# Attention, routed experts and an MLP on one core: paired bias operations, shorter GpSimd sums, and a planner that knows how TensorE's array is split

## The chip, the cores and the metric

One core of a Trainium2 chip runs the whole program in one launch. The metric is device time in microseconds (us), lower is better. Engines: PE is TensorE's matmul, PEld its weight load, DVE VectorE, ACT ScalarE, POOL GpSimd, SP SyncE (here it only issues DMAs).

## The reference

Three parts follow one another:

```python
proj = einsum('bhsd,md->bhsm', x, omega)            # x is q or k, scaled; b=4 h=8 s=576 d=64, m=128
h = proj - sum(x * x, -1, keepdims) / 2
phi = exp(h - max(h, -1, keepdims)) / sqrt(m)
kv, z = einsum('bhsm,bhsd->bhmd', phi_k, v), sum(phi_k, axis=2)
attn = einsum('bhsm,bhmd->bhsd', phi_q, kv) / (einsum('bhsm,bhm->bhs', phi_q, z)[..., None] + 1e-6)
# 2304 tokens of 512: each goes to the expert of its largest logit (8 experts, 512 -> 1024 -> 512, relu), times its gate
# then a dense layer 512 -> 2048, a piecewise quadratic, 2048 -> 512
```

## The kernel before

The program has an attention stage (to about 178 us), a sort of the tokens by expert, the experts, and the dense layers. The change lies in the first, in the step to the sort, and in one register load of the experts.

The attention stage is a list of tasks that class `Plan` puts in order when the program is built. Each task has an engine, a cost in ns, a rank, the tasks it comes after and the ring buffers it takes and uses. `run` keeps a clock for each engine and picks, again and again, the task that can start first (within `SLACK`, the lowest rank). What comes out is a fixed order for each engine; on the chip every engine works through its own in order and waits where an input is not there.

A block is 256 rows of q or k of one batch (8 heads, 2 rows a partition: 128x1024), or the last 64 rows of two batches (128x512, "small"): 20 blocks. `block_tasks` loads it, squares it (ACT for k, POOL for q), and adds up the 64 squares of each row on POOL in six halving additions (L424, L426) into `nsq`. A unit is four heads of a block: 36 units. `unit_tasks` transposes the unit (L449), copies it out of PSUM on ACT (L454), and multiplies with omega in four groups `project(c)` that use quarters of the array (64x64, L461) into two PSUM banks, one for each half `i` of the unit. For each half DVE takes the row maximum over 128 features (L468), then two small operations on 128x4 make the bias (L471, L475), and ACT runs four exponentials (L480). `kv_tasks` makes kv and z of four heads on halves of the array (64 columns, L506), `c_tasks` transposes the q features (L564), copies them and makes numerator, denominator and logits (L581, halves of the array) for a tile of 128 tokens, and `r_tasks` ranks the tokens of one or two tiles by expert, scales the rows and stores them to `xd` in HBM (L679 for the tile of the small blocks, L682 for the others). Transposes and the small ranking matmuls (L686 to L715) use the whole array. PSUM is one ring of 8 banks ("ps") for all of this.

After the plan, DVE sorts the experts by size (L856 to L896). `gather(0)` reads the rows of the first expert by index (three DMAs of POOL, L937); in the program it waits for every store to `xd` and for the index `gidx` (L724). `m_x0` transposes them, `m_split` makes two float parts on ACT and DVE, and `m_h`, `m_y` are the expert's two layers. ACT reads eight offsets from `ints` into registers (L926) ahead of the first split; each `yT` write uses one (L1002).

Of the kernel before, what the change touches and what calls it, by code (L numbers as in the profile page):

```python
# [18 lines left out]
P = 128  # L19
# [19 lines left out]
class Plan:  # L39

    SLACK = 10.0
    HOPS = {"PE": {"PE": 30.0, "ACT": 200.0, "DVE": 200.0, "POOL": 200.0, "SP": 200.0},
# [12 lines left out]

    def add(self, engine, cost, fn, rank, after=(), take=(), use=()):
        for b in use:  # L60
            b["uses"] += 1
        self.tasks.append((engine, cost, fn, rank, [a for a in after if a is not None], take, use))
        return len(self.tasks) - 1
# [4 lines left out]
    def run(self):  # L68
# [8 lines left out]
        at = {t[0]: 0.0 for t in self.tasks}  # L77
        order = []
        while open_:
            best = {}  # L80
            for i in open_:
                engine, _, _, rank, _, take, _ = self.tasks[i]
# [14 lines left out]
            start, _, i = pick  # L97
            engine, cost, fn, _, _, take, use = self.tasks[i]
            open_.remove(i)
# [56 lines left out]
def kernel(  # L156
# [144 lines left out]
    with ExitStack() as actx:  # L301
# [57 lines left out]
        def omega_tasks():  # L359
            pb = buf("ps")  # L360

            def load():
                for i in range(2):
                    nc.sync.dma_start(out=om2[:, i * HD:(i + 1) * HD], in_=omega)
                nc.sync.dma_start(out=cs[:, P:C_END], in_=consts[:, P:C_END])

            def turn():
                nc.tensor.transpose(at(pb)[:, 0, :], om2, ident)

            def scaled():  # L370
# [7 lines left out]
            x = add("PE", 110, turn, -5, after=[x], take=[pb])  # L378
            return add("ACT", 240, scaled, -5, after=[x], use=[pb])
# [15 lines left out]
        def block_tasks(which, blk, rank):  # L395
# [23 lines left out]
            def tree():  # L419
                nsq = ap.tile([P, 2 * H, 1], F32, name="nsq", tag="nsq", bufs=12)  # L420
# [6 lines left out]
                o["nsq"] = nsq[:, :, 0]  # L427

            f = 0.5 if small else 1.0
            sb = buf("sqt")  # L430
            o["load"] = add("SP", 1460 * f, load, rank - 8, take=[o["buf"]])
            if which == "k":
                t = add("ACT", 950 * f, lambda: square("ACT"), rank - 0.5, after=[o["load"]], take=[sb], use=[o["buf"]])
            else:
                t = add("POOL", 2300 * f, lambda: square("POOL"), rank - 0.5, after=[o["load"]], take=[sb],
                        use=[o["buf"]])
            o["sq"] = add("POOL", 3540 * f, tree, rank - 0.4, after=[t], use=[sb])
            return o

        def unit_tasks(u, o, rank, prev):
# [31 lines left out]
            def bias2(i):  # L474
                dve.scalar_tensor_tensor(out=r["bi", i], in0=r["sq", i], scalar=SQ, in1=r["mx", i],  # L475
                                         op0=ALU.mult, op1=ALU.subtract)

            def exps(i):
                for j in range(4):
                    act.activation(at(ppb)[:, 2 * j + i, :], at(pjb[i])[:, j, :], AF.Exp, bias=r["bi", i][:, j:j + 1])  # L480

            pjb = [buf("ps"), buf("ps")]
            ta = add("PE", 435, turn, rank - 1.5, after=[o["load"]] + prev, take=[ptb], use=[o["buf"], ptb])
# [4 lines left out]
            ends, tb = [], x  # L488
            for i in range(2):
                t = add("DVE", 600, lambda i=i: top(i), rank + 4.5, after=[tb, o["sq"]], use=[pjb[i]])  # L490
                t = add("DVE", 75, lambda i=i: bias1(i), rank + 1, after=[t])
                t = add("DVE", 75, lambda i=i: bias2(i), rank + 1, after=[t])
                ends.append(add("ACT", 1005, lambda i=i: exps(i), rank + 2, after=[t] + ends[0:1],
# [4 lines left out]
        def kv_tasks(b, hf, a, st, rank, vload):  # L498
# [38 lines left out]
            for h in range(4):  # L537
                t = add("PE", 640, lambda h=h: head(h), rank + 3 + 0.2 * h,
                        after=a[0]["done"] + a[1]["done"] + st["done"] + [vload, t], take=[kvb] if h == 0 else [],
                        use=bufs)  # L540
# [3 lines left out]
            t = add("PE", 216, turn, rank + 1.2, after=[c1], take=[p1], use=[kcb])  # L544
            t = add("ACT", 265, copy3, rank + 1.2, after=[t], take=[ktb], use=[p1])
            t = add("PE", 400, gates, rank + 1.3, after=[t, gload], take=[p2], use=[ktb])
            t = add("DVE", 100, copy4, rank + 1.3, after=[t], use=[p2])
# [3 lines left out]
        def c_tasks(t, us, kvs, rank):  # L551
# [55 lines left out]
            for hf in range(2):  # L607
                x = add("PE", 435, lambda hf=hf: turn(hf), rank + 3.5, after=done, take=[ptb[hf]], use=bufs)
                cp_.append(add("DVE" if hf else "ACT", 600 if hf else 480, lambda hf=hf: copy(hf), rank,
                               after=[x], take=[qtb[hf]], use=[ptb[hf]]))  # L610
            x = None
            for hf in range(2):
                y = add("PE", 560, lambda hf=hf: num(hf), rank + 0.5, after=[cp_[hf], x] + kvs,
                        take=[nmb[hf]], use=[qtb[hf]])
                x = add("ACT", 295, lambda hf=hf: copy_out(hf), rank + 1.5, after=[y, x], take=[] if hf else [nxb],
                        use=[nmb[hf]])
# [7 lines left out]
        def r_tasks(t0, cs_, rank, prev):  # L624
# [117 lines left out]
            for j in range(n):  # L742
# [6 lines left out]
                add("SP", 730, lambda j=j: store(j), rank - 4, after=[g], use=[xb[j]])  # L749
            x = add("PE", 35, count, rank + 0.3, after=[rs], take=[pb])  # L750
# [6 lines left out]
            x = add("PE", 142 * n, place, rank + 0.5, after=ws, take=[p2])  # L757
            places.append(x)
# [160 lines left out]
    with ExitStack() as mctx:  # L919
# [71 lines left out]
        def m_y(e, d, h):  # L991
# [3 lines left out]
            for f in range(8):  # L995
# [246 lines left out]
```

## Time and profile before

| | |
|---|---|
| time, median of 3 runs (lowest, highest) | 857.43 us (854.82, 857.69) |
| the profiled execution: its own time, span | 862.34 us, 860.5 us |
| busy: PE, PEld, DVE, ACT, POOL | 800.6, 719.0, 578.9, 360.7, 406.6 us |
| first matmul of the experts (L981) | at 191.85 us |

Busy time is what an engine's instructions cover; a busy PE is not a PE at its peak, since matmuls overlap and their ends are modelled. In the 40 slices of the profile's page PE has 8 or 9 tenths nearly everywhere but in slice 9 (172 to 194 us), which is the step from attention to the experts, and the granted clock is at five tenths there.

### The profile page before, as it was taken

What the parts mean: (1) busy time and instruction counts of PE and PEld (TensorE: products, weight loads), DVE (VectorE), ACT (ScalarE), POOL (GpSimd) and SP (SyncE); (2) the same over time, 40 slices, a digit from 0 to 9 for tenths busy, and PEclk for the clock granted to TensorE, in tenths of its full rate; (3) what the DMA queues carried; (4) which work ended last, traced back from release to release, by engine and by line L of the source; (5) the groups of instructions that cost most, each with busy time, mean ns of one, the idle gap of its engine ahead of it and who ended that gap; (6) DMA issues with size and microseconds to landing.
All of it is one profiled execution on the core that took longest, in us unless ns stands there. A gap on an engine that the chain in (4) does not pass through costs nothing.

```text
span 860.5 us, 17028 instructions
## 1 busy us (share of the span) xinstructions
PE 800.6 (93%) x6530; PEld 719.0 (84%) x6530; DVE 578.9 (67%) x1174; ACT 360.7 (42%) x890; POOL 406.6 (47%) x467
## 2 busy tenths in 40 slices
PE   6898999759999999979979999999999999999994
PEld 4676777629999999969869898999989999899993
DVE  3789996965557654634598776589667977746541
ACT  5887978602222222211244645444343344434321
POOL 6868782443444444152265543355344544333443
PEclk9999999959999999999999999999999999999998
DMA  9966201135555555474442111012001200001111
GB/s 221 219 156 169 88 36 28 51 108 170 156 172 170 177 161 171 84 173 147 150 156 90 50 37 38 26 50 74 26 25 50 74 26 1 1 13 50 50 49 62
DMA packets 79025, 80.72 MB, mean 94 GB/s; under 512 B 28896, under 2 KB 61792, under 8 KB 78932
## 3 DMA queue, kind: packets, MB, share of 16 engines
q1 hardware_dynamic: 74996, 68.10, 28.2%
q0 software_dynamic: 3120, 9.85, 3.4%
q10 hardware_dynamic: 816, 1.57, 0.5%
q8 instruction: 54, 0.88, 0.4%
q14 instruction: 39, 0.32, 0.1%
HBM read 70.06 MB, written 9.45 MB: 92 GB/s over the span
## 4 chain that ended last, share of the span: by engine, by line
PE 45%; DVE 3%; DMA 1%; issue 1%; POOL 1%; ACT 0%; POOLq 0%; DVEq 0%; SPq 0%; ACTq 0%
PE po L1181 8%; PE ph L1137 7%; PE ph L1135 7%; PE ph L1136 7%; PE po L1180 7%; PE po L1179 7%; DVE wy L260 1%; DVE yl L916 1%; DMA out_dram<-acc,oidx 1%; DMA wraw<-in_moe_w_dram 0%; POOL gl L1164 0%; DMA wraw<-in_moe_w_in_dram 0%; DVE wy L259 0%; DVE wl L274 0%; DVE wz L263 0%
## 5 line engine op out<-in xcount | busy, mean ns | idle before, releaser
L1164 POOL TENSOR_TENSOR gl<-cl,gh 128x384 fp32r<-128x384 f32 x96 | 102.6, 1091 | 161.9 <-ACT gh L1163 151.9
L1156 ACT ACTIVATE cl<-cl,half 128x384 f32<-128x384 f32 x96 | 56.9, 614 | 211.2 <-DVE cl L1155 211.2
L265 POOL TENSOR_SCALAR wh<-wraw 128x1024 fp32r<-128x1024 f32 x60 | 70.2, 1173 | 138.3 <-DMA wraw<-in_moe_w_dram 86.6
L1136 PE MATMUL ph<-yl,wh 128*128 128x384 f32 x384 | 128.9, 336 | 1.8 <-DVE yl L916 1.8
L1137 PE MATMUL ph<-yh,wl 128*128 128x384 f32 x384 | 129.0, 336 | 0.0
L1135 PE MATMUL ph<-yh,wh 128*128 128x384 f32 x384 | 128.9, 336 | 0.0
L1181 PE MATMUL po<-wh,gl 128*128 128x512 f32 x288 | 113.6, 394 | 0.5 <-POOL gl L1164 0.5
L1180 PE MATMUL po<-wl,gh 128*128 128x512 f32 x288 | 113.0, 392 | 0.0
L1179 PE MATMUL po<-wh,gh 128*128 128x512 f32 x288 | 112.2, 389 | 0.0
L1155 DVE TENSOR_SCALAR cl<-ph 128x384 f32<-128x384 f32 x96 | 51.4, 551 | 77.1 <-PE ph L1137 76.3
L274 DVE TENSOR_TENSOR wl<-wraw,wh 128x1024 fp32r<-128x1024 f32 x60 | 75.3, 1255 | 17.3 <-POOL wh L265 17.3
L981 PE MATMUL ph<-xh,wh 128*128 128x328 f32 (+7 forms) x256 | 81.4, 318 | 5.6 <-DVE hl L987 3.6
L480 ACT ACTIVATE pp<-ps,bi 128x128 f32<-128x128 f32 x288 | 82.1, 407 | 6.0 <-DVE bi L475 6.0
L916 DVE TENSOR_TENSOR yl<-yT,yh 128x384 fp32r<-128x384 f32 x96 | 80.9, 900 | 4.3 <-ACT yh L915 4.3
L999 PE MATMUL py<-hh,wh 128*128 128x328 f32 (+7 forms) x256 | 81.2, 317 | 1.7 <-ACT yT L1002 1.7
L982 PE MATMUL ph<-xl,wh 128*128 128x328 f32 (+7 forms) x256 | 80.0, 313 | 2.8 <-DVE xl L950 2.8
L1000 PE MATMUL py<-hl,wh 128*128 128x328 f32 (+7 forms) x256 | 78.4, 306 | 2.5 <-DVE hl L987 2.5
L983 PE MATMUL ph<-xh,wl 128*128 128x328 f32 (+7 forms) x256 | 79.6, 311 | 0.0
L1001 PE MATMUL py<-hh,wl 128*128 128x328 f32 (+7 forms) x256 | 78.6, 307 | 0.2 <-DVE wl L274 0.2
L1136 PEld LDWEIGHTS ph<-yl,wh 128*128 128x128 f32 x384 | 72.1, 188 | 3.9 <-DVE yl L916 2.1
L1135 PEld LDWEIGHTS ph<-yh,wh 128*128 128x128 f32 x384 | 72.2, 188 | 1.8
L1137 PEld LDWEIGHTS ph<-yh,wl 128*128 128x128 f32 x384 | 72.1, 188 | 0.0
(158 smaller groups left out, 1700.5 us busy)
## 6 DMA issues: line engine op xcount, KB each, us to landing
wraw<-in_moe_w_dram SPq DMA_DIRECT2D x57, 512.0 KB, 3.8
wraw<-in_moe_w_in_dram SPq DMA_DIRECT2D x16, 512.0 KB, 4.1
wraw<-in_moe_w_out_dram SPq DMA_DIRECT2D x16, 512.0 KB, 3.4
xd<-xr SPq DMA_DIRECT2D x17, 256.0 KB, 2.3
blk<-in_k_dram SPq DMA_DIRECT2D x8, 512.0 KB, 6.8
blk<-in_q_dram SPq DMA_DIRECT2D x8, 512.0 KB, 5.0
vm<-in_v_dram SPq DMA_DIRECT2D x16, 256.0 KB, 5.8
wra<-in_moe_w_dram SPq DMA_DIRECT2D x4, 512.0 KB, 4.8
```

What stands on the lines that cost most here:

```text
L480: act.activation(at(ppb)[:, 2 * j + i, :], at(pjb[i])[:, j, :], AF.Exp, bias=r["bi", i][:, j:j + 1])
L916: nc.vector.tensor_sub(yl, yT[d][:, c], yh.bitcast(F32))
L981: nc.tensor.matmul(ph, lhsT=wh[:, d, c], rhs=xh, start=(d == 0), stop=False)
L982: nc.tensor.matmul(ph, lhsT=wh[:, d, c], rhs=xl, start=False, stop=False)
L999: nc.tensor.matmul(py, lhsT=wh[:, a, c], rhs=hh, start=(f == 0), stop=False)
L1135: nc.tensor.matmul(ph[f], lhsT=wh[:, a, c], rhs=yh, start=(d == 0), stop=False)
L1136: nc.tensor.matmul(ph[f], lhsT=wh[:, a, c], rhs=yl, start=False, stop=False)
L1137: nc.tensor.matmul(ph[f], lhsT=wl[:, a, c], rhs=yh, start=False, stop=(d == 3))
L1164: nc.gpsimd.tensor_sub(gl, cl, gh.bitcast(F32))
L1179: nc.tensor.matmul(po, lhsT=gh[:, c], rhs=wh[:, a, :], start=(f == 0), stop=False)
L1180: nc.tensor.matmul(po, lhsT=gh[:, c], rhs=wl[:, a, :], start=False, stop=False)
L1181: nc.tensor.matmul(po, lhsT=gl[:, c], rhs=wh[:, a, :], start=False, stop=(f == 3))
```

## The change

Five edits. (1) The two maxima of a unit go into one 128x2x4 tile, and one pair of bias operations on 128x8 serves both halves; the exponentials of the first half now come after the maximum of the second. The sum of squares is awaited by the bias, and no longer by the maxima. (2) POOL makes only the first two halvings of the squares (64 to 16); a DVE sum over 16 (`total`) makes the rest. (3) Each PE task names its mode, "whole", "halves" or "quarters" of the array; the planner adds 95 ns where the mode changes. Some costs are new. (4) The tile of the small blocks is stored with two DMAs of 64 rows in place of one with two pieces of 64 rows. (5) The offsets are loaded one by one, just ahead of the first `yT` write of each expert but the first, whose offset is 0.

```diff
+    CHANGE = 95.0
-                start = max(at[engine], ready[i])
+                start = max(at[engine] + (self.CHANGE if mode and mode != now else 0.0), ready[i])
...
             def tree():
-                w = 32
-                while w > 1:
+                for w in (32, 16):
                     pool.tensor_add(t[:, :, 0:w], t[:, :, 0:w], t[:, :, w:2 * w])
-                    w //= 2
-                pool.tensor_add(nsq[:, 0:n, :], t[:, :, 0:1], t[:, :, 1:2])
+            def total():
+                o["nsq"] = ap.tile([P, 2 * H], F32, name="nsq", tag="nsq", bufs=12)
+                dve.reduce_sum(o["nsq"][:, 0:n], at(sb)[:, 0:n, 0:16], axis=AX)
...
-            o["sq"] = add("POOL", 3540 * f, tree, rank - 0.4, after=[t], use=[sb])
+            t = add("POOL", 2000 * f, tree, rank - 0.4, after=[t], use=[sb])
+            o["sq"] = add("DVE", 60 + 270 * f, total, rank - 0.3, after=[t], use=[sb])
...
-            def bias1(i):
-                dve.scalar_tensor_tensor(out=r["mx", i], in0=r["sq", i], scalar=SQ, in1=r["mx", i],
-                                         op0=ALU.mult, op1=ALU.add)
...
+            def bias():
+                sq = o["nsq"][:, 8 * hf:8 * hf + 8].rearrange("p (j i) -> p i j", i=2)
+                dve.scalar_tensor_tensor(out=r["mx"], in0=sq, scalar=SQ, in1=r["mx"], op0=ALU.mult, op1=ALU.add)
+                dve.scalar_tensor_tensor(out=r["bi"], in0=sq, scalar=SQ, in1=r["mx"], op0=ALU.mult, op1=ALU.subtract)
...
-                x = add("PE", 240, lambda c=c: project(c), rank + 1 + 0.1 * c, after=[x, setup],
-                        take=[] if c else pjb, use=[thb] + pjb)
+                x = add("PE", 220, lambda c=c: project(c), rank + 1 + 0.1 * c, after=[x, setup],
+                        take=[] if c else pjb, use=[thb] + pjb, mode="quarters")
...
-                    rows = xd[2 * it[1] * S:(2 * it[1] + 2) * S, :].rearrange("(i s) d -> i s d", i=2)
-                    nc.sync.dma_start(out=rows[:, 512:576, :], in_=x)
+                    for i in range(2):
+                        o = (2 * it[1] + i) * S + 512
+                        nc.sync.dma_start(out=xd[o:o + 64, :], in_=x[64 * i:64 * i + 64])
...
-        offs = [nc.scalar.value_load(ints[0:1, 0, e:e + 1], min_val=0, max_val=NT) for e in range(E)]
+        offs = {}
...
-            nc.scalar.activation(yT[d][:, bass.ds(offs[e], w)], py, AF.Copy)
+            if e and d == 0:
+                offs[e] = nc.scalar.value_load(ints[0:1, 0, e:e + 1], min_val=0, max_val=NT)
+            nc.scalar.activation(yT[d][:, bass.ds(offs[e], w)] if e else yT[d][:, 0:w], py, AF.Copy)
```

On PE, where the first batch's kv is made (ps are PSUM banks, vm and vs hold v, pp the k features, th a transposed unit; L506 is kv, L461 is projection), the order before is:

```order
L449 MATMUL ps_102<-cs,blk_114 128x128 x4
L506 MATMUL ps_101<-vm_148,pp_122 64x65 x4
L506 MATMUL ps_101<-vm_148,pp_124 64x65 x4
L506 MATMUL ps_101<-vs_150,pp_123 64x65 x2
L461 MATMUL ps_103<-oms,th_120 64x128
L461 MATMUL ps_102<-oms,th_120 64x128
L461 MATMUL ps_103<-oms,th_120 64x128
L461 MATMUL ps_102<-oms,th_120 64x128
L506 MATMUL ps_101<-vm_148,pp_122 64x65 x4
```

At the same place the order now is (kv is L508, the transpose of a unit L454):

```order
L454 MATMUL ps_104<-cs,blk_113 128x128 x4
L508 MATMUL ps_108<-vm_148,pp_122 64x65 x4
L508 MATMUL ps_108<-vm_148,pp_124 64x65 x4
L508 MATMUL ps_108<-vs_150,pp_123 64x65 x2
L508 MATMUL ps_108<-vm_148,pp_122 64x65 x4
L508 MATMUL ps_108<-vm_148,pp_124 64x65 x4
L508 MATMUL ps_108<-vs_150,pp_123 64x65 x2
```

The kv of a head alternated with a quarter of a projection; now the eight heads of both halves stand in one run. Over the attention stage PE's order has 202 changes of mode before and 76 now.

On DVE, the first two units of the program before (mx and bi are the maxima and the biases):

```order
L468 TENSOR_REDUCE mx<-ps_104 128x4
L468 TENSOR_REDUCE mx<-ps_105 128x4
L471 SCALAR_TENSOR_TENSOR mx<-nsq,mx 128x4 x2
L475 SCALAR_TENSOR_TENSOR bi<-nsq,mx 128x4 x2
L468 TENSOR_REDUCE mx<-ps_106 128x4
L468 TENSOR_REDUCE mx<-ps_107 128x4
L471 SCALAR_TENSOR_TENSOR mx<-nsq,mx 128x4 x2
L475 SCALAR_TENSOR_TENSOR bi<-nsq,mx 128x4 x2
```

and now:

```order
L431 TENSOR_REDUCE nsq<-sqt_116 128x16
L473 TENSOR_REDUCE mx<-ps_103 128x4
L431 TENSOR_REDUCE nsq<-sqt_117 128x8
L473 TENSOR_REDUCE mx<-ps_104 128x4
L477 SCALAR_TENSOR_TENSOR mx<-nsq,mx 128x8
L478 SCALAR_TENSOR_TENSOR bi<-nsq,mx 128x8
L473 TENSOR_REDUCE mx<-ps_106 128x4
L473 TENSOR_REDUCE mx<-ps_107 128x4
L477 SCALAR_TENSOR_TENSOR mx<-nsq,mx 128x8
L478 SCALAR_TENSOR_TENSOR bi<-nsq,mx 128x8
```

Four small operations of a unit became two, and the sums of squares of a block (L431) entered DVE's queue.

On SP, the last stores to xd before:

```order
L682 DMA xd<-xr_143 128x512
L682 DMA xd<-xr_141 128x512
L682 DMA xd<-xr_142 128x512
L679 DMA xd<-blk_111 2x64x512
```

and now:

```order
L685 DMA xd<-xr_143 128x512
L685 DMA xd<-xr_141 128x512
L685 DMA xd<-xr_142 128x512
L682 DMA xd<-blk_109 64x512 x2
```

Only the last store changed its shape.

## Rows read from the trace of the kernel before

**Rows 1.** Busy time by stage: start and end us, then each engine, PEclk, DMA share, GB/s.

```profile
20.00:158.00 138.00, 126.93 (x2471) 99.80 (x2471) 116.78 (x373) 117.67 (x379) 91.97 (x149) 0.99 0.45 111
158.00:178.00 20.00, 11.51 (x211) 9.38 (x210) 18.83 (x97) 7.84 (x24) 11.72 (x21) 0.85 0.25 95
178.00:192.00 14.00, 7.57 (x27) 3.65 (x25) 6.38 (x40) 0.64 (x2) 5.81 (x6) 0.62 0.30 86
192.00:860.50 668.50, 642.92 (x3672) 597.26 (x3672) 431.16 (x650) 224.39 (x465) 285.02 (x257) 0.99 0.28 87
```

**Rows 2.** Waits of PE from 20 to 158 us: total us, times, longest.

```profile
PE ps L581 <- DVE qt L570: 1.8, 1, 1.8
...
PE ps L461 <- DVE kvz L530: 0.4, 1, 0.4
```

**Rows 3.** Timeline of PE at two places: start us, us, instruction, count.

```profile
65.56 1.10 PE L461 MATMUL ps<-oms,th 64*64 64x128 f32 x32
66.59 0.18 PE L686 MATMUL ps<-rsb,oneb 128*128 128x16 bf16 x1
...
106.12 0.45 PE L461 MATMUL ps<-oms,th 64*64 64x128 f32 x8
106.50 0.73 PE L581 MATMUL ps<-kvz,qt 128*64 128x73 f32 x16
107.16 0.45 PE L461 MATMUL ps<-oms,th 64*64 64x128 f32 x8
```

**Rows 4.** Groups by line to 215 us: busy us, mean ns, idle before and releaser.

```profile
L468 DVE TENSOR_REDUCE mx<-ps 128x4 f32<-128x512 f32 x72 | 47.7, 681 | 16.7 <-PE ps L461 15.1 <-ACT kvt L522 1.2 <-issue 0.3
...
L475 DVE SCALAR_TENSOR_TENSOR bi<-nsq,mx 128x4 f32<-128x4 f32 x72 | 23.0, 338 | 0.2
L471 DVE SCALAR_TENSOR_TENSOR mx<-nsq,mx 128x4 f32<-128x4 f32 x72 | 22.5, 330 | 1.0 <-POOL nsq L426 1.0
...
L424 POOL TENSOR_TENSOR sqt<-sqt 128x128 f32<-128x128 f32 x20 | 10.0, 500 | 1.6
...
L602 DVE TENSOR_REDUCE lall<-lg 128x8 f32<-128x64 f32 x18 | 4.7, 263 | 0.3
```

**Rows 5.** Timeline of POOL and DVE around 105 us.

```profile
104.47 2.06 POOL L671 TENSOR_TENSOR xr<-nx,den 128x512 f32<-128x512 f32 x2 [0.56 <-DVE mx L471]
...
105.47 0.15 DVE L471 SCALAR_TENSOR_TENSOR mx<-nsq,mx 128x4 f32<-128x4 f32 x1
...
105.65 0.90 DVE L475 SCALAR_TENSOR_TENSOR bi<-nsq,mx 128x4 f32<-128x4 f32 x1
```

**Rows 6.** DMA from 170 to 190 us: GB/s in 0.5 us slices; stores, us to landing.

```profile
GB/s 0 0 0 0 0 287 238 287 238 0 209 315 0 0 25 25 45 12 33 49 41 49 57 49 66 49 41 0 0 0 0 0 0 123 336 115 213 221 123 180
...
xd<-xr SPq DMA_DIRECT2D x3, 256.0 KB, 2.0
```

**Rows 7.** Timeline from the last store to the first split of the experts.

```profile
176.00 0.52 SPq L679 DMA_DIRECT2D xd<-blk  x1
...
178.05 0.16 DVE L724 TENSOR_TENSOR gidx<-slots,ps 128x3 uint32<-128x3 f32 x1 [0.42 <-PE ps L854]
...
184.66 1.18 POOL L937 DMA_INDIRECT xg<-xd,gidx  x1 [7.90 <-DVE tsi L892]
...
184.83 0.18 DVE L896 CAST spos<-tsi 128x36 f32<-128x36 int32 x1
...
191.36 0.44 ACT L949 ACTIVATE xh<-px 128x328 fp32r<-128x328 f32 x1 [17.65 <-PE px L943]
```

**Rows 8.** ACT's offset loads: ns least, median, most; first and last start.

```profile
L926 ACTq TENSOR_LOAD <-ints x8: 277/280/477, 181.1 to 185.3; - x8
```

**Rows 9.** Timeline of ACT in the second expert: a write of yT.

```profile
242.01 0.40 ACT L1002 ACTIVATE yT<-py 128x272 f32 x1 [3.36 <-PE py L1001]
```

**Rows 10.** Busy time from 70 to 80 us, columns as in Rows 1.

```profile
70.00:80.00 10.00, 7.23 (x114) 5.78 (x116) 8.74 (x19) 6.57 (x19) 9.22 (x15) 0.83 0.72 182
```

**Rows 11.** Timeline of PE at 76 us.

```profile
76.00 0.79 PE L581 MATMUL ps<-kvz,qt 128*64 128x73 f32 x16 [1.76 <-DVE qt L570]
```

More of the change, by code (lines that the diff above doesn't have):

```diff
@@ L57, in buf, with add @@
         return {"ring": ring, "uses": 0, "end": 0.0}
-    def add(self, engine, cost, fn, rank, after=(), take=(), use=()):
+    def add(self, engine, cost, fn, rank, after=(), take=(), use=(), mode=None):
         for b in use:
             b["uses"] += 1
-        self.tasks.append((engine, cost, fn, rank, [a for a in after if a is not None], take, use))
+        self.tasks.append((engine, cost, fn, rank, [a for a in after if a is not None], take, use, mode))
         return len(self.tasks) - 1
@@ L78, in run @@
         order = []
+        now = None
         while open_:
@@ L81, in run @@
             for i in open_:
-                engine, _, _, rank, _, take, _ = self.tasks[i]
-                start = max(at[engine], ready[i])
+                engine, _, _, rank, _, take, _, mode = self.tasks[i]
+                start = max(at[engine] + (self.CHANGE if mode and mode != now else 0.0), ready[i])
                 for ring in {b["ring"] for b in take}:
@@ L97, in run @@
             start, _, i = pick
-            engine, cost, fn, _, _, take, use = self.tasks[i]
+            engine, cost, fn, _, _, take, use, mode = self.tasks[i]
+            now = mode or now
             open_.remove(i)
@@ L377, in omega_tasks @@
             add("DVE", 130, tri, 1, after=[x])
-            x = add("PE", 110, turn, -5, after=[x], take=[pb])
+            x = add("PE", 110, turn, -5, after=[x], take=[pb], mode="whole")
             return add("ACT", 240, scaled, -5, after=[x], use=[pb])
@@ L434, in block_tasks @@
             else:
-                t = add("POOL", 2300 * f, lambda: square("POOL"), rank - 0.5, after=[o["load"]], take=[sb],
+                t = add("POOL", 1900 * f, lambda: square("POOL"), rank - 0.5, after=[o["load"]], take=[sb],
                         use=[o["buf"]])
-            o["sq"] = add("POOL", 3540 * f, tree, rank - 0.4, after=[t], use=[sb])
+            t = add("POOL", 2000 * f, tree, rank - 0.4, after=[t], use=[sb])
+            o["sq"] = add("DVE", 60 + 270 * f, total, rank - 0.3, after=[t], use=[sb])
             return o
@@ L478, in exps @@
             def exps(i):
                 for j in range(4):
-                    act.activation(at(ppb)[:, 2 * j + i, :], at(pjb[i])[:, j, :], AF.Exp, bias=r["bi", i][:, j:j + 1])
+                    act.activation(at(ppb)[:, 2 * j + i, :], at(pjb[i])[:, j, :], AF.Exp, bias=r["bi"][:, i, j:j + 1])
             pjb = [buf("ps"), buf("ps")]
-            ta = add("PE", 435, turn, rank - 1.5, after=[o["load"]] + prev, take=[ptb], use=[o["buf"], ptb])
+            ta = add("PE", 435, turn, rank - 1.5, after=[o["load"]] + prev, take=[ptb], use=[o["buf"], ptb], mode="whole")
@@ L489, in unit_tasks @@
             for i in range(2):
-                t = add("DVE", 600, lambda i=i: top(i), rank + 4.5, after=[tb, o["sq"]], use=[pjb[i]])
-                t = add("DVE", 75, lambda i=i: bias1(i), rank + 1, after=[t])
-                t = add("DVE", 75, lambda i=i: bias2(i), rank + 1, after=[t])
+                t = add("DVE", 600, lambda i=i: top(i), rank + 4.5, after=[t], use=[pjb[i]])
+            t = add("DVE", 150, bias, rank + 1, after=[t, o["sq"]])
+            for i in range(2):
                 ends.append(add("ACT", 1005, lambda i=i: exps(i), rank + 2, after=[t] + ends[0:1],
@@ L537, in kv_tasks @@
             for h in range(4):
-                t = add("PE", 640, lambda h=h: head(h), rank + 3 + 0.2 * h,
+                t = add("PE", 570, lambda h=h: head(h), rank + 3 + 0.2 * h,
                         after=a[0]["done"] + a[1]["done"] + st["done"] + [vload, t], take=[kvb] if h == 0 else [],
-                        use=bufs)
+                        use=bufs, mode="halves")
                 heads.append(t)
@@ L543, in kv_tasks @@
             c2 = add("ACT", 270, copy2, rank + 1, after=[t], use=[kvb])
-            t = add("PE", 216, turn, rank + 1.2, after=[c1], take=[p1], use=[kcb])
+            t = add("PE", 216, turn, rank + 1.2, after=[c1], take=[p1], use=[kcb], mode="whole")
             t = add("ACT", 265, copy3, rank + 1.2, after=[t], take=[ktb], use=[p1])
-            t = add("PE", 400, gates, rank + 1.3, after=[t, gload], take=[p2], use=[ktb])
+            t = add("PE", 400, gates, rank + 1.3, after=[t, gload], take=[p2], use=[ktb], mode="whole")
             t = add("DVE", 100, copy4, rank + 1.3, after=[t], use=[p2])
@@ L607, in c_tasks @@
             for hf in range(2):
-                x = add("PE", 435, lambda hf=hf: turn(hf), rank + 3.5, after=done, take=[ptb[hf]], use=bufs)
+                x = add("PE", 435, lambda hf=hf: turn(hf), rank + 3.5, after=done, take=[ptb[hf]], use=bufs, mode="whole")
                 cp_.append(add("DVE" if hf else "ACT", 600 if hf else 480, lambda hf=hf: copy(hf), rank,
@@ L612, in c_tasks @@
             for hf in range(2):
-                y = add("PE", 560, lambda hf=hf: num(hf), rank + 0.5, after=[cp_[hf], x] + kvs,
-                        take=[nmb[hf]], use=[qtb[hf]])
+                y = add("PE", 510, lambda hf=hf: num(hf), rank + 0.5, after=[cp_[hf], x] + kvs,
+                        take=[nmb[hf]], use=[qtb[hf]], mode="halves")
                 x = add("ACT", 295, lambda hf=hf: copy_out(hf), rank + 1.5, after=[y, x], take=[] if hf else [nxb],
@@ L677, in store @@
                 if it[0] == "s":
-                    rows = xd[2 * it[1] * S:(2 * it[1] + 2) * S, :].rearrange("(i s) d -> i s d", i=2)
-                    nc.sync.dma_start(out=rows[:, 512:576, :], in_=x)
+                    for i in range(2):
+                        o = (2 * it[1] + i) * S + 512
+                        nc.sync.dma_start(out=xd[o:o + 64, :], in_=x[64 * i:64 * i + 64])
                 else:
@@ L749, in r_tasks @@
                 add("SP", 730, lambda j=j: store(j), rank - 4, after=[g], use=[xb[j]])
-            x = add("PE", 35, count, rank + 0.3, after=[rs], take=[pb])
+            x = add("PE", 60, count, rank + 0.3, after=[rs], take=[pb], mode="whole")
             x = add("DVE", 95, mine, rank + 2.3, after=[x], use=[pb])
@@ L756, in r_tasks @@
                 ws.append(add("DVE", 330, lambda j=j: one_b(j), rank + 0.4, after=[x, places[-1]]))
-            x = add("PE", 142 * n, place, rank + 0.5, after=ws, take=[p2])
+            x = add("PE", 160 * n, place, rank + 0.5, after=ws, take=[p2], mode="whole")
             places.append(x)
```

17 lines of the change are left out of this document (6 added, 11 removed).

## The prediction

> **What bounds the kernel now.** I read the busy time by stage first, then the waits of each engine in the attention stage, then single stretches of the timeline, and last the step from attention to the experts, wait by wait.
>
> From 192 us on PE is busy 642.92 of 668.50 us [rows 1], and no edit touches its work there. What the change can move is how early that part starts. From 20 to 158 us three engines are near each other: PE 126.93 of 138 us (92%), ACT 117.67 (85%), DVE 116.78 (85%), with POOL at 91.97 (67%) [rows 1]. PE waits little: twelve groups of waits, from 1.8 us down to 0.4, sum to 11.5 us [rows 2]. So PE is the queue that sets the pace, and ACT and DVE are 20 us behind it. From 158 to 178 us DVE is the bound, 18.83 of 20 us, on the ranking of the last tiles [rows 1]. From 178 to 192 us nearly nothing works: the last store is issued at 176.00, the index is written at 178.05, and the first gather starts at 184.66 [rows 7]. The row names DVE L892 as what it waited for, but the program lets it wait for the stores and for L724, which is long done. The store is still moving: in half-microsecond slices the three stores before it go at 209 to 315 GB/s, and then a trickle of 12 to 57 GB/s lasts for thirteen slices, from 177.0 to 183.5 [rows 6]. That trickle is the 256 KB of L679.
>
> **The change, part by part.**
>
> *Mode changes on PE.* A run of 32 projection loads takes 66.59 - 65.56 = 1.03 us to the next kind; a run of 8 takes 106.50 - 106.12 = 0.38 [rows 3]. Both hold one change c at their end, so with a for 8 loads 4a + c = 1.03 and a + c = 0.38: a = 0.22, c = 0.16. The order goes from 202 changes to 76, so PE is relieved of 126 x 0.15 = 18.9 us (0.15 to round down, since a change into the small ranking matmuls is cheaper). Bounds: 0.10 gives 12.6, 0.16 gives 20.2.
>
> *Bias and sums on DVE.* 144 operations of 338 and 330 ns go, 45.5 us [rows 4]. 72 on 128x8 come. The same operation takes 0.15 us where GpSimd leaves it alone and 0.90 beside a GpSimd multiplication [rows 5], and a mean of 0.33 is mostly that wait, so I price the new ones at 0.33: 23.8 us (bounds 0.15 and 0.34: 11 and 24.5). 20 sums over 16 come; no row has 128x256 into 16, and the neighbours are 263 ns for 64 elements and 681 for 512 [rows 4]. In proportion to elements that is 0.44 for 16 of them and 0.32 for the 4 small ones, 8.4 us (bounds 5.3 and 13.6). Net DVE -13 us. It buys no time by itself while PE sets the pace; it keeps DVE (to about 104) from taking PE's place.
>
> *GpSimd's levels.* The four short levels go, the largest of them 10.0 us [rows 4], some 25 us in all by the same group of lines. POOL has a third of the stage free, so this is priced at nothing; the cover is that free time. The new wait is the bias on the sum, and what stands behind a late sum is DVE's whole queue, the maxima of the next unit first. Before, that wait cost 1.0 us in all, once [rows 4]; with POOL less loaded I take 0.
>
> *Later exponentials.* The first half's exponentials now wait for the second maximum, 0.68 us, and the bank is held that much longer. With 36 units and two banks each that is some 0.4 us a bank more on about 4, against eight banks. Price 0 in the forecast; it is the seed of the slow rival.
>
> *What the attention stage gains.* If PE kept its 11.5 us of waits, the stage would shrink by the whole 18.9. But ACT's 117.67 us stay. The highest share that any engine holds in this stage is PE's 92%; at that share ACT needs 117.67 / 0.92 = 128 us. I take that: 138 to 128, -10 us. The ends are -18.9 and -2.
>
> *The tail of the stage.* Counted in PE's order, after the last projection there stood 6 groups of q transposes and 9 of numerators; now 10 and 14. That is work put off to where DVE and not PE is the bound: 9 groups at about 0.5 us (a group of 16 takes 107.16 - 106.50 = 0.66 with its change [rows 3]), 4.5 us if none hides, 0 if all does. I take +2.
>
> *The store.* The nearest row for a store that is one piece per row is xd<-xr, 2.0 us to landing [rows 6]. The second half is issued after the first, 0.52 us later at most [rows 7]: 176.0 + 0.5 + 2.0 = 178.5, against the end of the trickle at 183.5. The gather came 1.16 us after that end, so now at 179.7, 5.0 us earlier; no earlier than the index allows, so 5.4 at best, and 0 at worst if 64 rows move like two times 64. I take 4.5, with half a microsecond off because the gather's descriptors are now written while DVE sorts (to 184.83 + 0.18 [rows 7]).
> The trace has no store of 64 rows, so it can't say on how many DMA engines one spreads. The Trainium skill, "DMA: Bandwidth & Descriptors", "Why a DMA increments its semaphore by 16 and not by 1", says that the number of engines is the largest up to 16 that divides the slowest dimension of both sides: 2 for a target of 2x64 rows, 16 for 64. The trickle at a sixth of the other stores' rate agrees with the 2; by the rule the halves go like xr's stores, and the sum takes the 5.0, without it 0.
> What is late next is the split of the first expert: ACT's first xh at 191.36 waited 17.65 us for PE [rows 7], and moves with the gather.
>
> *The offset loads.* Eight of them, one every (185.3 - 181.1) / 7 = 0.6 us, held ACT from 181.1 to 185.6 or later [rows 8], inside that wait. With the gather 4.5 us earlier the first xh is due at 186.9, so leaving them there would still have just fit: 0 gained. Seven come back in the experts, ahead of a yT write that waits 3.36 us for PE [rows 9], which hides one of 0.6 us: 0. If the cover were gone, 7 x 0.6 = 4.2.
>
> *Sum.* -10 + 2 - 4.5 = -12.5 us on the profiled execution's 862.34 (1.8 more than its span): 849.8. That execution lies 0.6% above the median of the runs shown, 857.43, so the forecast in their terms is 857.43 x 849.8 / 862.34 = 845.
>
> **Rivals.**
>
> *PE alone was the limit (15%).* ACT and DVE waited for PE, not on their own account, and close up fully: -18.9 + 2 - 4.5 = -21.4, 836. For it: DVE's maxima wait 15.1 us on PE's projections, much of it at the start [rows 4]. Against it: ACT would have to be busy 117.67 of 119 us.
>
> *The gather doesn't come earlier (12%).* Either the halves are as slow as the whole, or descriptors starve while DVE sorts. -10 + 2 = -8: 849.5. For it: every gather of the trace but its first 0.2 us lay outside the sort, so none shows the overlap. The Trainium skill's "SBUF — State Buffer", "Who interferes with whom", speaks for this one: a DVE instruction in its two-port modes locks GpSimd out for its whole length, and descriptors of GpSimd's DMAs can't be written meanwhile. In this trace the sort's instructions take 0.15 to 0.3 us each, so by the rule the gather is delayed in short steps, at most to the sort's end at 185.0, where the 5.0 us would be gone.
>
> *The order brings nothing (8%).* Fixed queues of ACT and DVE, filled from costs, stay as loosely coupled as now: stage -2, tail +2, store -4.5: 853.
>
> *Long runs starve the other engines: slower (5%).* PE now makes kv of eight heads or two whole units in one run, and holds its banks longer. Where PE waited 1.76 us for DVE at 76.00 [rows 11], the granted clock fell to half soon after: 0.83 on average from 70 to 80 us [rows 10], so 0.17 x 10 x 2 = 3.4 us ran at 1.2 GHz and cost 1.7 us more. One such event costs 1.8 + 1.7 = 3.5 us. The gains are 18.9 + 4.5, less 2; from the seventh event on it is slower, and there are some 18 pairs of units in which it can happen. Eight give 862. Against it: so far it happens once in 138 us, with DVE fuller than it will be.
>
> **How the numbers follow.** The forecast has 60%. Its own range is 841 to 850: the stage between -6 and -14. At the start of the experts some 4 us run at half clock now; shifted, that is 2 us either way. To hold 8 in 10 the range reaches from 834, just past the first rival, to 855, past the third. Half a per cent, 4.3 us, is about what a measurement of this kernel tells from none, so faster means under 853.1: all of the forecast, the first two rivals and half of the third, less something for what I have not thought of: 0.86. Within half a per cent: 0.09. Slower: 0.05.
>
> **What would show it.** Mode changes: PE's busy time up to the end of the projections falls by 15 to 19 us. Stage: the last projection starts about 10 us earlier, and ACT's share rises past 90%; if PE's waits grow by much more than 9 us, ACT or the banks have taken over. Bias: L477 and L478 together near 24 us, the sums near 8. Store: no trickle after it, the first gather 1 to 2 us behind the index. Offsets: the loads inside waits of ACT for PE. Experts: from the first L984 to the end 668 to 670 us as now. The prediction is wrong if that last part changes by more than 3 us, or if the clock falls more than twice before the last projection.

## The result, and the profile after

The changed kernel takes 844.81 us (median of 4 runs, 841.62 to 849.25) against 857.56 us (4 runs, 854.82 to 859.41) for the kernel before: a ratio of 0.9853, 95% interval 0.9807 to 0.9899. The profiled execution took 845.65 us, its span 843.9; 845 was predicted.

The stages, with the stretches of [rows 1] (start and end us, then each engine, PEclk, DMA share, GB/s):

```profile
20.00:158.00 138.00, 120.10 (x2582) 105.20 (x2574) 116.00 (x359) 120.29 (x393) 74.62 (x88) 0.98 0.45 115
158.00:178.00 20.00, 10.46 (x95) 6.03 (x95) 16.39 (x95) 2.17 (x7) 11.41 (x17) 0.66 0.35 114
178.00:192.00 14.00, 12.94 (x75) 12.56 (x76) 6.88 (x11) 3.68 (x9) 5.03 (x6) 0.88 0.58 189
```

The stretch from 178 to 192 us, in which PE had 7.57 us of work, is now filled: the experts have begun. From the end of the last store on, the timeline answers to [rows 7]:

```profile
168.19 1.09 SPq L682 DMA_DIRECT2D xd<-blk  x2
169.39 0.16 DVE L727 TENSOR_TENSOR gidx<-slots,ps 128x3 uint32<-128x3 f32 x1 [0.42 <-PE ps L857]
...
172.10 1.17 POOL L940 DMA_INDIRECT xg<-xd,gidx  x1 [3.64 <-DVE u L871]
...
176.17 0.18 DVE L899 CAST spos<-tsi 128x36 f32<-128x36 int32 x1
...
178.92 0.44 ACT L952 ACTIVATE xh<-px 128x328 fp32r<-128x328 f32 x1 [12.98 <-PE py L946]
179.41 0.42 PE L984 MATMUL ph<-xh,wh 128*128 128x328 f32 x1 [0.47 <-ACT xh L952]
```

The index comes 8.7 us earlier (178.05 to 169.39), the first gather 12.6 us (184.66 to 172.10), the first matmul of the experts 12.44 us (191.85 to 179.41). The gather follows the index by 2.71 us, where it was 6.61, and runs while DVE still sorts.

All engines before and after, cut just behind the start of the last projection (156.36 us before, 142.15 now) and at the index, columns as in [rows 1]; first before, then after:

```profile
0.00:156.50 156.50, 137.68 (x2607) 107.95 (x2607) 121.00 (x382) 126.75 (x398) 103.35 (x182) 0.99 0.52 126
156.50:178.00 21.50, 12.48 (x239) 10.12 (x227) 20.33 (x104) 8.87 (x28) 12.42 (x23) 0.86 0.23 88
```

```profile
0.00:142.40 142.40, 119.52 (x2511) 104.08 (x2511) 112.55 (x317) 119.83 (x377) 80.17 (x102) 0.98 0.58 138
142.40:169.40 27.00, 18.09 (x330) 15.25 (x323) 23.87 (x119) 14.62 (x49) 11.90 (x23) 0.82 0.19 71
```

The projections end 14.2 us earlier, but the rest of the stage grew from 21.5 to 27 us: 5.6 us of PE's work and 5.75 of ACT's now lie behind the last projection.

The groups that the change touches on DVE, to 180 us, answer to [rows 4] (busy us, mean ns, idle before and releaser):

```profile
L473 DVE TENSOR_REDUCE mx<-ps 128x4 f32<-128x512 f32 x72 | 46.8, 681 | 7.3 <-PE ps L466 7.2
L477 DVE SCALAR_TENSOR_TENSOR mx<-nsq,mx 128x8 f32<-128x8 f32 x36 | 12.7, 353 | 0.3
...
L478 DVE SCALAR_TENSOR_TENSOR bi<-nsq,mx 128x8 f32<-128x8 f32 x36 | 11.8, 328 | 1.2
...
L431 DVE TENSOR_REDUCE nsq<-sqt 128x16 f32<-128x256 f32 (+1 forms) x20 | 7.6, 384 | 8.4 <-POOL sqt L427 8.4
```

The biases take 24.5 us and the sums 7.6. New is what stands behind the last bar: DVE waits 8.4 us for GpSimd ahead of the sums, where it waited 1.0 us before.

### The profile page after: what moved, and what is told of

It is laid out like the page before. It is cut to its first block, busy times and chain, and to the rows that moved or that the text cites. A ratio compares the mean times of both kernels' runs of the same rounds, so it can differ in the third digit from the quotient of the medians.

```text
span 843.9 us, 16906 instructions
## 1 busy us (share of the span) xinstructions
PE 786.3 (93%) x6530; PEld 719.0 (85%) x6530; DVE 577.7 (68%) x1122; ACT 359.9 (43%) x890; POOL 379.0 (45%) x387
## 4 chain that ended last, share of the span: by engine, by line
PE 47%; DVE 3%; DMA 1%; POOL 1%; issue 1%; ACT 0%; POOLq 0%; DVEq 0%; ACTq 0%
PE po L1186 8%; PE ph L1142 8%; PE ph L1140 8%; PE ph L1141 8%; PE po L1185 7%; PE po L1184 7%; DVE wy L265 1%; DVE yl L919 1%; DMA out_dram<-acc,oidx 1%; DMA wraw<-in_moe_w_in_dram 1%; PE ph L984 0%; PE ph L985 0%; PE ph L986 0%; POOL gl L1169 0%; DVE wy L264 0%
## 5 line engine op out<-in xcount | busy, mean ns | idle before, releaser
L270 POOL TENSOR_SCALAR wh<-wraw 128x1024 fp32r<-128x1024 f32 x60 | 67.5, 1126 | 137.8 <-DMA wraw<-in_moe_w_dram 85.9
L482 ACT ACTIVATE pp<-ps,bi 128x128 f32<-128x128 f32 x288 | 84.3, 472 | 6.6 <-DVE bi L478 6.6
```

## The experiments

Each kernel was timed over five rounds beside the kernel before. "Ratio" is to that kernel; "index" is the start of `gidx`, "clock" PE's mean granted clock from 20 to 140 us, both from the one profiled execution.

| kernel | ratio (95%) | index, us | clock |
|---|---|---|---|
| before | 1 | 178.05 | 0.99 |
| after | 0.9853 (0.9807 to 0.9899) | 169.39 | 0.97 |
| s1: after, one store | 0.9906 (0.9872 to 0.9940) | 169.31 | 0.96 |
| s2: before, two stores | 0.9927 (0.9905 to 0.9948) | 178.98 | 0.97 |
| m2: after, edit 3 undone | 0.9924 (0.9901 to 0.9947) | 176.01 | 0.97 |
| m3: before, edit 3 alone | 0.9978 (0.9954 to 1.0002) | 176.14 | 0.93 |
| b1: after, edit 2 undone | 0.9941 (0.9920 to 0.9963) | 179.42 | 0.93 |
| b2: after, edit 1 undone | 0.9914 (0.9888 to 0.9939) | 173.15 | 0.97 |
| o1: after, edit 5 undone | 0.9848 (0.9825 to 0.9872) | 173.07 | 0.94 |
| m4: after, 150 ns a change | 0.9914 (0.9880 to 0.9947) | 174.56 | 0.93 |
| m5: after, 110 ns a change | 0.9942 (0.9917 to 0.9967) | 174.87 | 0.97 |
| f1: after's order, two biases | 0.9892 (0.9853 to 0.9931) | 172.13 | 0.96 |
| f2: after's order, GpSimd sums | 0.9963 (0.9944 to 0.9982) | 176.91 | 0.91 |
| f3: after's order, one level | 0.9880 (0.9849 to 0.9911) | 168.91 | 0.94 |

A tenth of a per cent is 0.86 us.

### The store: s1 and s2

```diff
-                    for i in range(2):
-                        o = (2 * it[1] + i) * S + 512
-                        nc.sync.dma_start(out=xd[o:o + 64, :], in_=x[64 * i:64 * i + 64])
+                    rows = xd[2 * it[1] * S:(2 * it[1] + 2) * S, :].rearrange("(i s) d -> i s d", i=2)
+                    nc.sync.dma_start(out=rows[:, 512:576, :], in_=x)
```

s1 is this on the kernel after; s2 is the reverse on the kernel before.

> The kernel after, with the tile of the small blocks stored by one DMA with two pieces of 64 rows again (edit 4 undone), all else kept; the order of PE is the same. Theory: the slow trickle comes back, some 7 us from its issue at about 168.2 us to 175.5, and the first gather starts 1.2 us behind it, at 176.7 in place of 172.1: 844.8 + 4.6 = 849.4 us. Rival (the gather was early because the stage before it was shorter, and the store is hidden beside the sort): the gather stays near 172 to 173, 845 us.

> The kernel before, with edit 4 alone. Theory: no trickle, both halves land within 3 us of 176.0, the first gather at 179.2 to 179.7 in place of 184.66: 857.6 - 5 = 852.6 us. Rival (GpSimd's descriptors cannot be written while DVE sorts the experts, so the gather still starts near 185): 857.6 us.

Measured: s1 0.9906, 4.6 us above after; the two intervals overlap, so that here the traces decide. The DMA of s1 and then of after, in half-microsecond slices from 165 us:

```profile
GB/s 0 0 0 0 0 274 250 0 25 16 41 16 33 45 41 49 49 57 49 49 49 4 0 0 0 0 0 106 246 189 156 254 139 164 90 131 287 156 164 262
```

```profile
GB/s 0 0 0 0 0 217 307 0 106 184 213 21 0 0 0 0 0 25 156 320 98 123 303 82 172 123 156 270 148 246 189 127 188 369 377 365 348 385 397 381
```

In s1 the trickle is back, 16 to 57 GB/s from 169.0 to 175.5 us, and the gather starts at 176.81; after, the same bytes are through in four slices. In s1's trickle (169.0 to 175.5 us) the DMA share is 0.12, worth about two engines of 16; in after's four slices it is 0.59. The index is the same (169.31, 169.39), so the 4.5 us between the first matmuls of the experts (183.94, 179.41) are the store's alone. s2 gains 0.7%, 6.3 us, with 4.5 to 8.2 in the interval; in its profile the gather follows the index by 1.86 us (178.98, 180.84) while the sort goes on. Both rivals, hidden store and starved descriptors, fall.

### The order of PE: m2 and m3

m2 sets `CHANGE` to 0 and PE's costs to those of before; m3 is the kernel before with edit 3 alone:

```diff
-    CHANGE = 95.0
+    CHANGE = 0.0
...
-                x = add("PE", 220, lambda c=c: project(c), rank + 1 + 0.1 * c, after=[x, setup],
+                x = add("PE", 240, lambda c=c: project(c), rank + 1 + 0.1 * c, after=[x, setup],
```

> The kernel after, with edit 3 undone (no price for a change of mode, PE's costs of before): 195 changes of mode in PE's order in place of 76; edits 1, 2, 4, 5 stay. Theory (the stage got shorter because PE changes mode less often): PE's busy time to the last projection rises by 119 x 0.15 = 18 us, the index comes 8 to 9 us later, near 178, time 844.8 + 8.7 = 853.5 us. Rival (the relief of DVE and GpSimd by edits 1 and 2 made the stage shorter): the index stays near 170, 845 to 847 us.

> The kernel before, with edit 3 alone (71 changes of mode in place of 202); bias, sums, store and offset loads as before. Theory: PE is relieved by 131 x 0.15 = 19.6 us and the index comes 8 to 9 us earlier, near 169.5; the store's trickle stays: 857.6 - 8.7 = 848.9 us. Rival (without the relief of DVE and GpSimd these two hold the stage where it is): 855 to 858 us.

Measured: m2 0.9924, m3 0.9978. Without edit 3 the time is 6.1 us above after, where the theory had 8.7. But m2 equals s2 (0.9924, 0.9927): edits 1, 2 and 5, in the order that the planner makes without edit 3, bring nothing beyond the store. And edit 3 alone brings 1.9 us, not 8.7, in an interval that includes 1: the rival. That PE has less to do in the new order is shown; that it is through sooner is not. From 20 to 140 us, m2, after and m3:

```profile
20.00:140.00 120.00, 110.81 (x2164) 87.29 (x2158) 96.81 (x273) 103.47 (x331) 63.29 (x69) 0.97 0.50 123
20.00:140.00 120.00, 104.66 (x2269) 91.89 (x2262) 100.78 (x295) 105.44 (x344) 69.45 (x76) 0.97 0.51 127
20.00:140.00 120.00, 103.44 (x2150) 90.57 (x2150) 96.44 (x303) 101.94 (x333) 85.87 (x139) 0.93 0.49 123
```

At the same clock of 0.97, after does 105 matmuls more than m2 in 6.15 us less of PE's time. In these 120 us the kernel before has 109.46 us of PE at a clock of 0.99. m3 needs 6 us less for as many instructions (2152 and 2150), but 0.07 of 120 us, 8.4 us of full-speed work, is missing in its clock, against 1.2 before and 3.6 after. PE's waits, the longest of m3:

```profile
PE ps L720 <- DVE ob L712: 3.7, 2, 3.1
PE ps L691 <- ACT pp L485: 1.9, 1, 1.9
PE ps L466 <- DVE kvz L535: 1.8, 1, 1.8
```

So the order relieves PE, and in m3 PE stands idle more than before (16.6 us of the 120, against 10.5) and runs at half clock more often. But after has 15.3 us of idle PE too, and f3 below ends level with after at a clock of 0.94, so neither alone shows why m3 gains so little; that stays open. Store (0.73%), order (0.22%) and relief (0) alone make 0.95%; together they make 1.5%.

### Which relief: b1 and b2, and the planner's part: m4 and m5

b1 puts all six levels of the sum back on GpSimd, b2 puts two bias operations back for each half, both with the planner's costs of these steps as before, so that the order is planned anew. m4 and m5 change one number:

```diff
-    CHANGE = 95.0
+    CHANGE = 150.0
```

> The kernel after, with all six levels of the sums on GpSimd again (edit 2 undone, the paired bias stays); 72 changes of mode. DVE has 8 us less to do, GpSimd 25 us more. Theory P (what lets the new order of PE pay is DVE's relief by the pairing): nothing is lost, ratio to before 0.984 to 0.988. Theory S (GpSimd's short levels slow DVE's small operations and hold the bias): the mean of the bias operations rises above the 0.34 us of after, and half of the 6 us that edit 3 lacked without help is lost: ratio 0.989 to 0.994.

> The kernel after, with two bias operations for each half again (edit 1 undone, the sums split between GpSimd and DVE as after); 75 changes of mode. DVE has 72 operations of 0.33 us more, 22 to 24 us. Theory P: DVE becomes the queue that PE waits for, the granted clock falls more often, and the gain of the order is gone: ratio 0.991 to 0.995. Theory S: the pairing is worth nothing: ratio 0.984 to 0.988.

> The kernel after, with 150 ns for a change of mode in the planner in place of 95 (the 0.15 us that the prediction took as its real cost); 71 changes in place of 76. Theory (the planner gains by true costs): 5 x 0.15 = 0.75 us less for PE and a plan that drifts less, ratio 0.982 to 0.985. Rival (the order is sensitive: any other order of the same quality moves the index by some microseconds): a ratio between 0.983 and 0.993, with the granted clock at half in other places.

> The kernel after, with 110 ns for a change of mode in the planner in place of 95: 77 changes in place of 76, the order differs from about the fortieth part of the stage on. Theory L (two orders of equal quality by the planner's own measure lie up to 6 us apart on the chip, so that the 0.985 of after is in part luck): a ratio of 0.987 to 0.993. Rival (orders of equal count are equal, and 150 ns was worse because of its longer runs): 0.984 to 0.987.

Measured: b1 0.9941, b2 0.9914, m4 0.9914, m5 0.9942. b1 and b2 alone would say that each relief is needed (theory P is out for b1, theory S for b2). But m4 and m5 have every edit and as few changes of mode (71 and 77, where after has 76), and lose 5.2 and 7.7 us all the same. The planner's order is one draw among many, and draws of equal count differ by as much as the parts that were to be told apart. So the losses of b1 and b2 can't be put down to their edits. Nor can the 6.1 us between m2 and after, or the little that m3 gains, be put down to edit 3, since m2 and m3 were planned anew too: what the new order of PE is worth in time, no run here shows. Parts can be told apart only by kernels that keep the order.

### The same order: f1, f2 and f3

Here every task keeps its place; only what stands inside the bias or the sum differs. f1 makes the biases of the halves apart:

```diff
-                dve.scalar_tensor_tensor(out=r["mx"], in0=sq, scalar=SQ, in1=r["mx"], op0=ALU.mult, op1=ALU.add)
+                for i in range(2):
+                    dve.scalar_tensor_tensor(out=r["mx"][:, i, :], in0=sq[:, i, :], scalar=SQ, in1=r["mx"][:, i, :],
+                                             op0=ALU.mult, op1=ALU.add)
```

f2 makes `tree` six levels again and `total` empty; f3 goes the other way:

```diff
-                for w in (32, 16):
-                    pool.tensor_add(t[:, :, 0:w], t[:, :, 0:w], t[:, :, w:2 * w])
+                pool.tensor_add(t[:, :, 0:32], t[:, :, 0:32], t[:, :, 32:64])
...
-                dve.reduce_sum(o["nsq"][:, 0:n], at(sb)[:, 0:n, 0:16], axis=AX)
+                dve.reduce_sum(o["nsq"][:, 0:n], at(sb)[:, 0:n, 0:32], axis=AX)
```

> The kernel after, with exactly its order of tasks on every engine; only inside the bias step of a unit the pair of operations on 128x8 is again two pairs on 128x4 (72 more DVE operations, at 0.15 to 0.33 us: 11 to 24 us). Theory P (DVE is near the bound once PE is relieved): the last projection 4 to 10 us later, ratio to before 0.990 to 0.997. Rival L (the loss of the kernel with edit 1 undone, 0.9914, came from its other order): with the order kept nothing is lost, 0.984 to 0.988.

> The kernel after, with exactly its order of tasks; only the work of the sums is shifted back: all six levels on GpSimd, none on DVE. GpSimd has 25 us more, DVE 20 operations (8 us) less. Theory C (GpSimd has that room, as the prediction said): 0.982 to 0.988, and the wait of DVE for a sum moves into the bias. Rival (the sum arrives later by the four short levels, 1.3 us and more each, and DVE's queue stands behind it): 0.990 to 0.997.

> The kernel after, with exactly its order of tasks; GpSimd makes only the first halving of the squares (64 to 32), and the DVE sum takes 32 in place of 16. GpSimd has 18 us less (20 levels of 0.84 us and less), DVE some 5 us more (512 elements at 0.68 us in place of 256 at 0.41). With the same order and all six levels on GpSimd the ratio was 0.9963, with two levels 0.985. Theory R (the time goes with how late GpSimd hands on the sum): DVE's waits for it shrink from 6.8 us to about 4, ratio 0.980 to 0.984. Rival D (DVE is the next limit: 11 to 24 us more of small operations in the same order gave 0.9892): 0.986 to 0.989.

Measured: f1 0.9892, between the two expectations. Its 144 biases take 31.2 us, 6.7 more than after, and about 3.4 us of time are lost; the intervals of f1 and after overlap, so that this is likely rather than shown.

f2 0.9963, 9.5 us above after with intervals far apart: with the order kept, the four short levels on GpSimd cost more than all edits but the store bring together (8.1 us by s1). The biases are not slower for it (24.3 us in f2, 24.5 after). The first place where f2 falls behind is at 55 us. GpSimd and DVE of after:

```profile
51.14 2.09 POOL L427 TENSOR_TENSOR sqt<-sqt 128x512 f32<-128x512 f32 x2 [9.09 <-ACT sqt L420]
53.17 1.90 POOL L422 TENSOR_TENSOR sqt<-blk 128x1024 f32<-128x1024 f32 x1
```

```profile
53.45 0.41 DVE L431 TENSOR_REDUCE nsq<-sqt 128x16 f32<-128x256 f32 x1
53.78 0.68 DVE L473 TENSOR_REDUCE mx<-ps 128x4 f32<-128x512 f32 x1
54.38 0.72 DVE L477 SCALAR_TENSOR_TENSOR mx<-nsq,mx 128x8 f32<-128x8 f32 x1
...
59.09 0.17 DVE L652 TENSOR_TENSOR ohall<-req,rmm 128x16 bf16<-128x16 f32 x1
```

and of f2:

```profile
51.95 3.35 POOL L429 TENSOR_TENSOR sqt<-sqt 128x512 f32<-128x512 f32 x5 [6.05 <-ACT sqt L420]
55.38 0.22 POOL L431 TENSOR_TENSOR nsq<-sqt 128x16 f32<-128x16 f32 x1
55.55 1.89 POOL L422 TENSOR_TENSOR sqt<-blk 128x1024 f32<-128x1024 f32 x1
```

```profile
55.63 1.84 DVE L481 SCALAR_TENSOR_TENSOR mx<-nsq,mx 128x8 f32<-128x8 f32 x1 [0.75 <-POOL nsq L431]
57.50 0.97 DVE L482 SCALAR_TENSOR_TENSOR bi<-nsq,mx 128x8 f32<-128x8 f32 x1
...
61.44 0.17 DVE L656 TENSOR_TENSOR ohall<-req,rmm 128x16 bf16<-128x16 f32 x1
```

Five levels take 3.35 us where two take 2.09. The bias waits 0.75 us for the sum, starts just as GpSimd's next multiplication starts, and takes 1.84 us beside it in place of 0.72. Everything in DVE's queue is 2.35 us later up to the ranking (`ohall`), of which 0.8 us was there when GpSimd began; and PE's matmul of the ranks waits for it. After and f2:

```profile
59.51 0.18 PE L689 MATMUL ps<-rsb,oneb 128*128 128x16 bf16 x1 [1.12 <-DVE rsb L655]
```

```profile
61.87 0.18 PE L693 MATMUL ps<-rsb,oneb 128*128 128x16 bf16 x1 [2.66 <-DVE rsb L659]
61.91 0.17 PE L695 MATMUL ps<-ohall,trib 128*128 128x16 bf16 x1
61.93 2.24 PE L570 MATMUL ps<-cs,pp 128*128 128x128 f32 x12
```

The 12 transposes behind it take 2.24 us in f2, where they take 1.51 after, and from 60 to 70 us the granted clock is at the lower level, 1.2 GHz, for part of the time (0.83 on average, 1.00 after).

Part of this was made up: at the transposes of the next units (71.79 us after, 73.82 in f2) PE is 2.0 us late. Most of the loss comes at two later places of the same kind, where the bias waits 1.71 and 2.39 us for the sum. The same biases after, and then in f2:

```profile
74.29 0.16 DVE L477 SCALAR_TENSOR_TENSOR mx<-nsq,mx 128x8 f32<-128x8 f32 x1
...
113.45 0.15 DVE L477 SCALAR_TENSOR_TENSOR mx<-nsq,mx 128x8 f32<-128x8 f32 x1
```

```profile
76.20 0.99 DVE L481 SCALAR_TENSOR_TENSOR mx<-nsq,mx 128x8 f32<-128x8 f32 x1 [1.71 <-POOL nsq L431]
...
119.89 0.17 DVE L481 SCALAR_TENSOR_TENSOR mx<-nsq,mx 128x8 f32<-128x8 f32 x1 [2.39 <-POOL nsq L431]
```

Behind the first, PE's matmul of the ranks is 3.7 us late (80.38 and 84.08). The maxima ahead of the second are 4.8 us late (107.45 and 112.22), the kv behind it 7.1 us (116.97 and 124.07), and the index comes 7.5 us later than after's. From 20 to 140 us f2's clock is 0.91 on average: up to 10.8 us of full-speed work missing, against 3.6 after. How much of f2's loss that is, no run shows.

f3 0.9880, with an interval that overlaps after's, while its profiled execution is after's to the tenth (span 843.9, index 168.91): not told apart from after, though the ratio lies in the range of rival D. DVE's waits for the sum fell to 4.8 us as theory R had it, and in the end no gain from this or from GpSimd's 18 us shows: a lead of 2.5 us at the maxima of 93 us (90.42, after 92.95) was gone at 107 us (107.44 and 107.45), with a clock of 0.68 from 90 to 106 us where after has 0.89. The total of these waits does not tell their cost: it is 8.4 us after, 4.9 in f2 and 4.8 in f3, and f2 alone is clearly slower. By these profiles it is where they fall. After's longest cost nothing: f2, which does not wait for the sum at this place, makes its next maximum no earlier. After, and then f2:

```profile
31.35 0.42 DVE L431 TENSOR_REDUCE nsq<-sqt 128x16 f32<-128x256 f32 x1 [4.08 <-POOL sqt L427]
32.52 0.69 DVE L473 TENSOR_REDUCE mx<-ps 128x4 f32<-128x512 f32 x1 [0.75 <-PE ps L466]
```

```profile
32.65 0.69 DVE L477 TENSOR_REDUCE mx<-ps 128x4 f32<-128x512 f32 x1 [5.44 <-ACT kvz L519]
```

### The offset loads: o1

The list of eight loads goes back ahead of the first split:

```diff
+        offs = [nc.scalar.value_load(ints[0:1, 0, e:e + 1], min_val=0, max_val=NT) for e in range(E)]
...
-            if e and d == 0:
-                offs[e] = nc.scalar.value_load(ints[0:1, 0, e:e + 1], min_val=0, max_val=NT)
```

> The kernel after, with the eight offset loads together ahead of the first split (edit 5 undone). Theory (hidden on both sides): the loads run from about 172.5 to 177 us, and ACT's first xh is due at 178.9; ratio as after, 0.985, within 0.001. Rival 1 (the loads in the experts were not hidden): 7 x 0.6 = 4.2 us faster, 0.980. Rival 2 (the loads together hold the first xh): up to 2 us slower, 0.988.

Measured: 0.9848 (0.9825 to 0.9872), equal to after, as expected; 0.980 and 0.988, the two rivals, lie outside. Up to the sort o1 has after's order and tasks, so its narrower interval can stand for after's: m2, m4, m5 and f2 lie clear of it, s1's begins where it ends, and those of f1 and f3 overlap it. None of the other kernels is below 0.988, so there is no better version among them.

## Why the prediction was right, and where it was not

The total was right, 844.81 for 845, and so was its sum to the first expert: -12.5 us predicted, -12.44 measured. Single terms were not, and two errors cancelled. This is luck in part: the prediction put the whole gain of the stage down to mode changes, with the paired biases to keep it, and by f2 it would not have been there, in this order, without GpSimd's relief, which was priced at nothing. Of the gains, only the store's is shown by runs of its own.

- **Mode changes (-18.9, bounds 12.6 to 20.2): mis-sized.** PE's busy time to the last projection fell by 18.2 us, as the sign I had named, but 5.6 of it was put off behind the projection. Over the whole stage it fell from 150.16 to 137.61 us, 12.6, or 0.10 us a change. More of after's time was at half clock: at full clock its PE would have up to 7.7 us less (0.02 x 142.4 + 0.18 x 27), before's up to 4.6, which lifts this to 0.125 at most. The 0.16 from two runs of loads was too much, and no row or run shows that a change into the ranking matmuls is cheaper, the reason given for 0.15. The time that this relief brings by itself is not shown.
- **Stage (-10) and tail (+2): measured -14.2 and +5.5.** The step that failed is "ACT's 117.67 us stay". That was the work in a stretch; 5.75 us of it moved past the last projection, where I had counted nine PE groups but no ACT behind them. ACT's share became 88% (107.84 of 122.4 us from 20 us on), not over 90. The sum, -8.7 for -8, came out near because the two errors have opposite signs.
- **GpSimd's levels (0): wrong.** "A third of the stage free" was no cover. The free time of an ordered queue lies where it waits, and the levels lay between a square and a bias that DVE's whole queue stood behind. f2 prices them at 9.5 us. A wait of PE followed by the lower clock, as in the rival "long runs starve the others", is seen in f2 (2.66 us, then 0.83), there behind a late sum. (Eight of that rival's events give 864 by its own terms, not 862.)
- **The wait of the bias on the sum (0): measured 8.4 us** ahead of the sum. f3, with 4.8, shows no gain, so the 0 in the sum held though the wait grew.
- **DVE's sizes: right.** 24.5 us for 23.8, 7.6 for 8.4. That pairing buys nothing by itself agrees with m2 against s2, and that it keeps DVE from taking PE's place with f1; neither is shown, since m2 has an order of its own and f1's interval overlaps after's.
- **Store (-4.5): right.** Gap from index to gather -3.9, alone 4.5 (s1). The halves land 2.3 us after their issue, with 2.0 assumed. The Trainium skill, "DMA: Bandwidth & Descriptors", "Why a DMA increments its semaphore by 16 and not by 1", which gave the 64-row halves all engines and the 2x64 target two, agrees with s1's trickle, at a DMA share worth about two engines of 16, and with after's four slices. (The trickle before reached 66 GB/s, not 57; nothing hangs on it.) Of the starvation that the Trainium skill's "SBUF — State Buffer", "Who interferes with whom", warns of, nothing shows: from gather to first xh it is 6.82 us beside the sort, and was 6.70 behind it.
- **Offset loads (0): right** (o1).
- **Experts "668 to 670 as now": missed**, 664.5: a change of 4.2 us, where the prediction called itself wrong beyond 3. The runs put this down to before's profiled execution, not to the change: from the first matmul of the experts to the first of the dense layers it took 255.12 us, with a wait of 2.8 us for `xl`; after 251.25, and s2 and m3, with before's code there and without that wait, 250.94 and 249.90. The other such sign did not come: the clock fell twice before the last projection (0.66 from 80 to 85 us and from 94 to 99), not more often.

What I could not see, and gave no chance of its own, is that the gain hangs on the one order that 95 ns gives. By the ratios of m4 and m5, the same edits at 150 or 110 ns give 850.1 and 852.5 us (of 857.5): still in the range, but by the path of a rival.

## What to carry to other kernels

When a planner fixes the order of four queues, undoing an edit also draws a new order: keep the order and change the work inside the tasks, or time a few neighbouring constants, before an edit is called good or bad. Spare time of an engine covers its work only if it lies where that work is; look at what stands ahead of it and who waits behind. The total of a wait does not price it. A strided target of few outer rows deserves a look at its DMA's GB/s: splitting one store was the cheapest and surest part of this gain.

## What the hardware showed

- Two operations of 128x8 on DVE take 0.17 us each alone (at 59.11 in f2), and 1.84 us where one stands beside a GpSimd multiplication of 1.89 us.
- The same order in the same stage took 142.15, 142.07 and 145.81 us to the last projection in three profiled executions (after, s1, o1), the slowest with the lowest mean clock (0.97, 0.96, 0.94).
- In m3, m4, b1 and f2, where PE had less to do and the time did not follow, the granted clock averaged 0.91 to 0.93 from 20 to 140 us, against 0.99 in the kernel before. But b2 and m5 lost time at 0.97, and f3 ended level with after at 0.94 (a span of 843.9 us in both): the mean clock of this stretch does not by itself tell how long a kernel takes.
